# Query halves of an attention kernel kept in the queries' interleaved order and read with a stride, with the order of attention written out anew

## The chip, the cores and the metric

The kernel runs on one core of a Trainium2 chip. The metric is the device time of one execution in microseconds. The core has TensorE (matrix products), VectorE, ScalarE, GpSimd and SyncE (which issues DMAs); in the rows they are PE (PEld for its weight loads), DVE, ACT, POOL and SP. Each engine executes its instructions in the order of the program.

## The reference

Three stages follow one another. The attention is a delta rule with a state S of 48 x 48 for each of 4 x 8 = 32 pairs of batch and head, over 768 steps:

```
k_n = k / (|k| + 1e-6)
for t in range(768):
    y[t] = q[t] @ S
    S = S + beta[t] * outer(k_n[t], v[t] - k_n[t] @ S)
```

Its output, as 3072 tokens of 384 values, goes through a mixture of 8 experts (each token to the best one of them, 384 to 1024 to 384, times its gate), and then through a dense layer 384 to 2048 to 384 with ELU between.

## The kernel before

Attention is cut into 12 chunks of 64 steps. The 32 pairs are taken two at a time: with 64 steps of one pair and 64 of another on the 128 partitions, a pair of pairs u = 0 to 15 is one block-diagonal matrix. Float32 values are split into a float16 high part and a float16 low part (value minus high), and a product is made of three: high x high, high x low, low x high.

For each chunk c the program does this. `lane(c)` scales k, splits it (khi, klo), copies it into the block-diagonal tile bdK, transposes it with TensorE into KTc, copies that into bdKT, makes the masked Gram matrix Lc = KT x KT (`gram`, kind gramL), and copies it into bdL. `invert(g)` inverts the diagonal blocks of two chunks on GpSimd (30 small steps) and puts the result into bdT by DMA. `rest(c)` loads v and q, scales q by 32, splits it into Qc (high and low) and makes the second Gram matrix Ac = KT x Q (`gram`, gramA, plain). `chain(c, hb)` is the recurrence, for each half hb of the pairs: it evicts a residual R into rh (ScalarE or VectorE, kind evac, L1082 or L1083), multiplies by bdT, evicts z, forms the residual with bdL, four times over, and then updates the state. `outputs(c, hb)` copies the state and z into bdS and bdZ, multiplies them with Qc and Ac, and evicts yT; `to_rows` transposes yT into tokens. After every two chunks `route` picks the experts and scatters the tokens with indirect DMAs (GpSimd, L341), 24 in all. After attention the expert stage and the dense layer follow, with a program and an order of their own.

The query tile in SBUF, `raw`, comes with its pairs interleaved: 4 blocks b, 64 steps i, 4 pairs u, u innermost. Qc of before has one contiguous run of 64 steps for each pair, so the split reorders: in `rest` the source is read through `um` with a step of four float32 values. These lines do it (L1320 makes the high half, L1321 the low half on GpSimd, L1323 the scaled low half on VectorE in four instructions):

```
fu = um(q.rearrange("p (b i u) -> p b i u", b=4, u=4))
hi, lo = (Qc[:P112, x].rearrange("p (b u) i -> p b u i", u=4) for x in range(2))
```

TensorE then reads a pair's 64 steps through `un(t, part, u)`, which is contiguous. The other tiles keep an interleave: `at(t, part, u)` reads KTc, Lc, Zc, Sc, bdKT, bdL, bdT with a step of two float16 values, Kc and bdK with a step of four.

The order is written out. Every operation is one of 2,280 entries of a plan. For each there may be several ways (another engine, or a DMA); the string WAYS[kind] has one digit for each operation of the kind, and STARTS has one number for each entry, by which `replay` sorts all entries; each engine then executes its entries in this order, and the four PSUM banks `pw` are handed out in it. So nothing is planned at run time, and the figures of cost beside the operations have no effect on the program while STARTS has as many numbers as there are entries. For the block-diagonal copies (`bd`, two halves each) the digit is 0 for a DMA of SyncE's queue, 1 for VectorE, 2 for ScalarE, 3 for GpSimd. For evac and shi 0 is ScalarE and 1 VectorE. For query the digit picks a triple: who multiplies by 32, who makes the high half, who makes the low half.

Of the kernel before, what the change touches and what calls it, by code (L numbers as in the profile page):

```python
# [199 lines left out]
class Moe(Ops):  # L200
# [92 lines left out]
    def route(self, a, xt, first, step, last):  # L293
# [51 lines left out]
        for b in tiles:  # L345
            x, g = xt[:, b, :DM], self.gs[:, b:b + 1]
            a.op("gate", ("ACT", DM + 155, lambda x=x, g=g: nc.scalar.activation(out=x, in_=x, func=AF.Copy, scale=g)),
                    ("DVE", DM - 130, lambda x=x, g=g: dv.tensor_scalar(out=x, in0=x, scalar1=g, scalar2=None, op0=ALU.mult)), r=["gs"], w=[f"xt{b}"])
            a.pl.add("POOL", 1.04, lambda b=b: scatter(b), r=[f"xt{b}", "di", f"xid{b}", "xz", *xs], move=0.55)
        if not last:  # L350
            xi = xt.bitcast(I32)[:, part, DM]
            a.pl.add("POOL", 0.1, lambda: nc.gpsimd.tensor_scalar(out=xi, in0=xi, scalar1=128, scalar2=None, op0=ALU.add), w=[f"{x}{b}" for b in tiles for x in ("xid", "xt")])
# [600 lines left out]
C = 64  # L953
# [58 lines left out]
class Attn(Ops):  # L1012
# [7 lines left out]
    def __init__(self, ctx, tc, plan, kt, vt, qt, beta, ident, zeros, lend):  # L1020
# [24 lines left out]
        self.Ac, self.Qc = til("Ac", [128, 2, NP, C]), many("Qc", [128, 2, NP, C], NQ)  # L1045
# [46 lines left out]
    def clear(self, names, t, after=(), due=()):  # L1092
# [6 lines left out]
                ("DVE", n, lambda: nc.vector.memset(f, 0.0)),  # L1099
# [66 lines left out]
    def gains(self, c0, c1, keep=False):  # L1166
# [4 lines left out]
        for c in range(c0, c1):  # L1171
            k, kn = self.load_k(c)
            q, qn = k, kn
            if keep:
# [3 lines left out]
                    ("POOL", 874, lambda k=k, q=q: nc.gpsimd.tensor_tensor(out=q, in0=k, in1=k, op=ALU.mult)),  # L1178
# [10 lines left out]
    def bd(self, dst, dn, src, sn, rows, cols=C):  # L1189
# [4 lines left out]
        for h in range(2):  # L1194
# [6 lines left out]
                              ("POOL", 0.185 + m * 0.0012, lambda o=oc, i=ic: nc.gpsimd.tensor_copy(o, i), 0.0)])  # L1201
# [4 lines left out]
    def gram(self, c, dst, dn, mov, mn, kind, plain=False):  # L1206
# [4 lines left out]
        col = un if plain else at  # L1211
        for hb in range(2):
# [24 lines left out]
            buf = self.pe(0.68, prod, r=[*two(f"bdKT{c % NT_}"), *mn], after=[nh, nl], take="pw")  # L1237
# [59 lines left out]
    def rest(self, c):  # L1297
# [14 lines left out]
        fu = um(q.rearrange("p (b i u) -> p b i u", b=4, u=4))  # L1312
        hi, lo = (Qc[:P112, x].rearrange("p (b u) i -> p b u i", u=4) for x in range(2))
        if c == NC_ - 1:
            hi, lo, fu = um(hi), um(lo), um(fu)
# [139 lines left out]
    def outputs(self, c, hb):  # L1455
# [29 lines left out]
        if c:  # L1485
            buf = self.pe(0.68, state, r=["bdSa", "bdSb", *qn, *ar], after=["yT"], take="pw")
# [36 lines left out]
    "bd": "1002000120202202022020110122120110002100001000030000000011022001000201010000000100111000000111000010000002000021100000002303030010000010000130300232030000001011",  # L1523
    "clear": "1012101110132103211200",
    "dg": "000000100110000101100001001000000010000000100000",
    "evac": "000100000100000010000001001000000001010101000110010000001001100000101000000101001001000000100100000011110000000000000010101000000000011101001010110111000010110001011110011110100100000000000001",
    "gate": "000010011010001011111111",
    "gramA": "715064030343250603356405",
    "gramL": "310011071602163015661356",
    "invert": "111111",  # L1530
    "kgain": "000100101110",
    "khi": "000011010010",
    "klo": "010100000001",
    "last": "001000221000220011002100",
    "lput": "111010101001110010111101",
    "norm": "000001100000",
    "query": "212121105515",
    "shi": "1100000000000010011001",
    "square": "002000120011",
    "turn": "101101001000000000101100000000000011000101010010",  # L1540
    "value": "101010121010",
    "whi": "0001011",
    "wlow": "0011000",
    "xput": "100010010100100010001000",
    "xsq": "001000000010100000101000",
# [188 lines left out]
```

## Time and profile before

| | |
|---|---|
| time, median of 3 runs (lowest to highest) | 990.22 us (988.76 to 990.22) |
| the profiled execution: time, span | 988.69 us, 986.9 us |
| TensorE busy | 852.7 us (86% of the span) |
| VectorE busy | 775.1 us (79%) |
| ScalarE busy | 600.0 us (61%) |
| GpSimd busy | 434.8 us (44%) |
| TensorE's granted clock, mean | 0.951 |

The span is the time from the first to the last instruction in the profile; the execution's time lies 1.8 us above it. Busy time is the time in which an engine executes an instruction; waits for semaphores are not in it. The granted clock is a share of TensorE's full speed, 2.4 GHz.

### The profile page before, as it was taken

The numbers are of one execution on the slowest core, as the hardware profiler recorded it, in microseconds if no ns is written. First come the engines' busy times: TensorE is split into PE (matmuls) and PEld (weight loads), VectorE is DVE, ScalarE is ACT, GpSimd is POOL, SyncE is SP. The second block draws the span as 40 slices with busy tenths as digits, with TensorE's granted clock in tenths as the row PEclk, the third lists the DMA queues.
The fourth block names the chain that finished last, engine by engine and source line by source line (L and its number), as shares of the span: only waits on it lengthen the run. The fifth ranks groups of instructions, "written<-read, shape, count | busy, mean of one in ns | idle before, by whom it ended". The sixth has DMA issues, their size and how long they took to land.

```text
span 986.9 us, 28916 instructions
## 1 busy us (share of the span) xinstructions
PE 852.7 (86%) x11783; PEld 711.4 (72%) x11784; DVE 775.1 (79%) x1631; ACT 600.0 (61%) x1077; POOL 434.8 (44%) x635
## 2 busy tenths in 40 slices
PE   0448888788798785699999999989999999999995
PEld 0436786678687674355556566879999999999995
DVE  7887887778687774577899797997778777878874
ACT  9786777767685851465566644765545555555662
POOL 6465464665556322123233421355446362355452
PEclk9957999899899987799999999999999999999998
DMA  6658874747653523967799526401010100100000
GB/s 204 158 117 234 226 154 93 147 110 130 136 112 89 176 65 106 242 141 235 223 222 210 189 80 127 125 18 49 18 49 17 48 19 1 49 17 18 18 17 18
DMA packets 122103, 108.79 MB, mean 110 GB/s; under 512 B 79753, under 2 KB 107181, under 8 KB 121709
## 3 DMA queue, kind: packets, MB, share of 16 engines
q1 hardware_dynamic: 115885, 84.84, 35.5%
q0 software_dynamic: 6080, 22.05, 6.9%
q8 instruction: 94, 1.54, 0.7%
q14 instruction: 44, 0.36, 0.1%
HBM read 74.19 MB, written 19.97 MB: 95 GB/s over the span
## 4 chain that ended last, share of the span: by engine, by line
PE 52%; DVE 4%; issue 2%; DMA 1%; SPq 0%; ACT 0%; POOL 0%; POOLq 0%; ACTq 0%; DVEq 0%
PE pa L648 18%; PE acc L668 15%; PE acc L606 10%; PE pa L587 9%; DMA xr<-xs_scratch 1%; DVE wbl L662 1%; DVE w L512 1%; PE pa L559 0%; PE pa L555 0%; DVE w L511 0%; DVE y L616 0%; DVE wal L654 0%; DVE wbl L466 0%; SPq L542 0%; DVE x L564 0%
## 5 line engine op out<-in xcount | busy, mean ns | idle before, releaser
L668 PE MATMUL acc<-dbh,wbl 128*128 128x192 f16 x672 | 165.3, 246 | 0.0
L668 PE MATMUL acc<-dbh,wbh 128*128 128x192 f16 x672 | 165.3, 246 | 0.0
L668 PE MATMUL acc<-dbl,wbh 128*128 128x192 f16 x672 | 165.3, 246 | 0.0
L648 PE MATMUL pa<-x,dah 128*128 128x256 f16 x1152 | 158.2, 274 | 3.1 <-DVE wal L654 2.5
L648 PEld LDWEIGHTS <-dah 128*128 128x128 f16 x1152 | 112.5, 98 | 16.4 <-issue 3.6
L668 PEld LDWEIGHTS <-wbh 128*128 128x128 f16 x1344 | 122.0, 98 | 1.2
L648 PE MATMUL pa<-x,dal 128*128 128x256 f16 x576 | 95.0, 274 | 0.0
L587 PE MATMUL pa<-x,wah 128*128 128x440 f16 (+6 forms) x384 | 77.5, 338 | 0.6 <-DVE hl L601 0.4
L1204 PEld LDWEIGHTS <-bdKT 112*128 112x128 f16 x1680 | 58.6, 102 | 19.9 <-issue 14.2
L1204 PEld LDWEIGHTS <-bdL 128*128 128x128 f16 x1536 | 55.9, 101 | 21.9 <-issue 15.7
L661 ACT CAST wbh<-wah 128x384 f16<-128x384 f32 (+1 forms) x88 | 49.3, 561 | 34.9 <-PE acc L668 12.0
L600 ACT ACTIVATE hh<-pa 128x440 f16<-128x440 f32 (+6 forms) x64 | 32.1, 505 | 58.3 <-PE acc L606 34.0
L668 PEld LDWEIGHTS <-wbl 128*128 128x128 f16 x672 | 65.7, 98 | 0.1
L1204 PEld LDWEIGHTS <-bdK 128*128 128x128 f16 x960 | 40.9, 119 | 33.6 <-DVE bdK L1200 14.3
L606 PE MATMUL acc<-hh,wbh 128*128 128x440 f16 (+6 forms) x192 | 64.1, 334 | 0.0
L655 POOL TENSOR_TENSOR wal<-wal 128x128 f32<-128x128 f32 (+1 forms) x65 | 43.1, 663 | 47.6 <-DVE wal L655 23.1
L606 PE MATMUL acc<-hl,wbh 128*128 128x440 f16 (+6 forms) x192 | 64.1, 334 | 0.0
L606 PE MATMUL acc<-hh,wbl 128*128 128x440 f16 (+6 forms) x192 | 64.1, 334 | 0.0
L655 POOL TENSOR_TENSOR wah<-wah 128x128 f32<-128x128 f32 (+1 forms) x62 | 37.0, 597 | 58.2 <-DVE wah L655 33.5
L661 ACT CAST wbh<-wal 128x384 f16<-128x384 f32 (+1 forms) x74 | 42.2, 571 | 32.8 <-PE acc L668 16.6
L648 PEld LDWEIGHTS <-dal 128*128 128x128 f16 x576 | 56.7, 98 | 6.9 <-DVE dal L527 0.2
L1204 PE MATMUL R<-z,bdL 128*128 128x48 f16 x1536 | 58.8, 189 | 2.7 <-issue 2.1
(323 smaller groups left out, 2370.3 us busy)
## 6 DMA issues: line engine op xcount, KB each, us to landing
st<-in_w SPq DMA_DIRECT2D x24, 512.0 KB
st<-in_w SPq DMA_DIRECT2D x32, 384.0 KB
kraw<-in_k SPq DMA_DIRECT2D x22, 384.0 KB
w<-in_w_in POOLq DMA_DIRECT2D x12, 512.0 KB, 4.6
w<-in_w_out POOLq DMA_DIRECT2D x16, 384.0 KB, 3.4
xs_scratch<-in_zeros SPq DMA_DIRECT2D x8, 675.5 KB
raw<-in_q SPq DMA_DIRECT2D x12, 448.0 KB
vraw<-in_v SPq DMA_DIRECT2D x12, 384.0 KB
```

Of the source, the lines that this page charges most:

```text
L512: self.dve(n, lambda m=m, lo=lo: v.scalar_tensor_tensor(out=m, in0=lo, scalar=29, in1=m, op0=ALU.logical_shift_right, op1=ALU.bitwise_or), ...
L587: self.nc.tensor.matmul(self.pa[i][:, :n], lhsT=W[w][:, k, c], rhs=x[:, k, y, t0:t0 + n], start=j == 0 and k == 0, stop=j == 2 and k == 2)
L600: self.act(cap, lambda i, hh=hh: nc.scalar.activation(out=hh, in_=self.pa[i][:, :cap], func=AF.Relu), w=[hn], buf=buf)
L606: nc.tensor.matmul(self.acc[d][:, :cap], lhsT=w[:, f, c], rhs=h, start=f == 0 and j == 0, stop=f == 7 and j == 2)
L648: nc.tensor.matmul(o, lhsT=D[w][:, k, c], rhs=x[:, k, y, t0:t0 + 256], start=q + n + k == 0, stop=n + k == 4, skip_group_check=True)
L655: add = lambda o, x, y, op: [(e, n, lambda w=w: w.tensor_tensor(out=o, in0=x, in1=y, op=op)) for e, n, w in (("POOL", o.shape[1] * 128, nc ...
L661: self.op("ghi", ("ACT", n, lambda f=f, fh=fh: nc.scalar.copy(fh, f)), ("DVE", n / 2, lambda f=f, fh=fh: v.tensor_copy(fh, f)), r=[gn + z] ...
L662: self.op("glow", *((e, n * c, lambda f=f, fh=fh, fl=fl, w=w: w.tensor_tensor(out=fl, in0=f, in1=fh, op=ALU.subtract)) for e, c, w in (("D ...
L668: nc.tensor.matmul(self.acc[k][:, o:o + HD], lhsT=h[:, u - 1], rhs=D[d][:, p, w - 1], start=p == 0 and n == 0 and o == FIRST[k], stop=p == ...
L1204: self.nc.tensor.matmul(o, lhsT=l, rhs=r, start=st, stop=True, skip_group_check=True)
```

## The change

Qc keeps the queries' own order, [4 blocks, 64 steps, 4 pairs]. Both halves are then written contiguously, from a contiguous source, and the scaled low half on VectorE is one instruction and not four. TensorE reads a pair's 64 steps at a step of four float16 values, through the new helper `by4`, in gramA (576 products) and in the output products with bdS (528 products). The list of query ways is another: without an own multiplication, with a high half on ScalarE or VectorE; and with one on GpSimd, ScalarE or VectorE, with a low half on GpSimd. The strings WAYS and the numbers STARTS of attention are new throughout; by count the strings say:

| kind | before | after |
|---|---|---|
| bd (160 half copies) | DMA 100, VectorE 31, ScalarE 21, GpSimd 8 | DMA 79, VectorE 32, ScalarE 28, GpSimd 21 |
| query, high half | ScalarE 12 | ScalarE 12 |
| query, low half | GpSimd 9, VectorE 3 (scaled) | GpSimd 8, VectorE 4 (scaled) |
| evac (192) | ScalarE 136, VectorE 56 | ScalarE 143, VectorE 49 |
| shi (22) | ScalarE 16, VectorE 6 | ScalarE 20, VectorE 2 |
| yout (24) | ScalarE 17, VectorE 7 | ScalarE 13, VectorE 11 |
| klo (12) | GpSimd 9, VectorE 3 | GpSimd 7, VectorE 5 |

The first two digits of bd are chunk 0's copies into bdK (before DMA for the second, after ScalarE), the next two those into bdKT. The other edits are figures of cost (such as 1.04 to 1.33 for a scatter). The core of the diff, without the lists of numbers, the strings of the other kinds and most figures of cost:

```diff
@@ -997,6 +997,11 @@
     return t[:, part, u]
 
 
+def by4(t, part, u):
+
+    return t[:, part, u // 4, :, u % 4]
+
+
 def un4(t):
     return t.rearrange("p (b u) i -> p b u i", u=4)
 
...
@@ -1042,7 +1047,7 @@
         self.lent = [f"{n}{x}" for n in ("bdK2", "bdK3", "bdK4", "bdKT0", "bdL0", "bdL1") for x in "ab"]
         self.lent += ["Kch", "Kcl"] + [f"{n}{hb}{x}" for n in ("KTc", "Lc") for hb in range(2) for x in "hl"]
         self.Zc = til("Zc", [128, 8, 2, C, 2])
-        self.Ac, self.Qc = til("Ac", [128, 2, NP, C]), many("Qc", [128, 2, NP, C], NQ)
+        self.Ac, self.Qc = til("Ac", [128, 2, NP, C]), many("Qc", [128, 2, 4, C, 4], NQ)
         self.Sc = many("Sc", [128, 8, 2, C, 2], 2)
         self.vraw = til("vraw", [128, NP, D], F32)
         self.bdS, self.bdZ = (til(n, [128, 4, 2, 128, 2]) for n in ("bdS", "bdZ"))
...
@@ -1208,7 +1213,7 @@
 
         nc, bdKT = self.nc, self.bdKT[c % NT_]
         self.pl.part = (kind, c)
-        col = un if plain else at
+        col = by4 if plain else at
         for hb in range(2):
             hs = slice(4 * hb, 4 * hb + 4)
             us = slice(hb * HB, (hb + 1) * HB)
...
@@ -1234,7 +1239,7 @@
                 mv = um(oh)
                 f = dst[:, hs].rearrange("p b l i u -> p (b l) (i u)")
                 m16 = self.mask.rearrange("p i u -> p (i u)")[:, None, :].to_broadcast([128, 8, 2 * C])
-            buf = self.pe(0.68, prod, r=[*two(f"bdKT{c % NT_}"), *mn], after=[nh, nl], take="pw")
+            buf = self.pe(0.78 if plain else 0.68, prod, r=[*two(f"bdKT{c % NT_}"), *mn], after=[nh, nl], take="pw")
             key = self.pl.number(kind)
             act = lambda o: ("ACT", 512, lambda i: nc.scalar.copy(o, pv(i)))
             dve = lambda o: ("DVE", 512, lambda i: nc.vector.tensor_copy(o, pv(i)))
...
@@ -1309,19 +1314,18 @@
         self.load(lambda: nc.sync.dma_start(out=q, in_=self.qt[c]), 370e3, w=["raw"])
         f = q
 
-        fu = um(q.rearrange("p (b i u) -> p b i u", b=4, u=4))
-        hi, lo = (Qc[:P112, x].rearrange("p (b u) i -> p b u i", u=4) for x in range(2))
-        if c == NC_ - 1:
-            hi, lo, fu = um(hi), um(lo), um(fu)
+        hi, lo = (Qc[:P112, x].rearrange("p b i u -> p (b i u)") for x in range(2))
         by = {"POOL": ("POOL", 1024, lambda: nc.gpsimd.tensor_tensor(out=f, in0=f, in1=self.sx[:P112].to_broadcast([P112, NP * C]), op=ALU.mult)),
               "ACT": ("ACT", 1024, lambda: nc.scalar.activation(out=f, in_=f, func=AF.Copy, scale=SX)),
               "DVE": ("DVE", 512, lambda: nc.vector.tensor_scalar(out=f, in0=f, scalar1=SX, scalar2=None, op0=ALU.mult)),
               "NONE": ("NONE", 0, lambda: None)}
-        high = {"ACT": ("ACT", 2300, lambda: nc.scalar.copy(hi, fu)), "NONE": ("ACT", 2300, lambda: nc.scalar.activation(out=hi, in_=fu, func=AF.Copy, scale=SX))}
-        low = {"POOL": ("POOL", 1310, lambda: nc.gpsimd.tensor_tensor(out=lo, in0=fu, in1=hi, op=ALU.subtract)),
-               "DVE": ("DVE", 1930, lambda: nc.vector.tensor_tensor(out=lo, in0=fu, in1=hi, op=ALU.subtract)),
-               "NONE": ("DVE", 1930, lambda: [nc.vector.scalar_tensor_tensor(out=lo[:, b], in0=fu[:, b], scalar=SX, in1=hi[:, b], op0=ALU.mult, op1=ALU.subtract) for b in range(4)])}
-        ways = [(by[a], high["NONE" if a == "NONE" else "ACT"], low[b]) for a, b in (("POOL", "POOL"), ("ACT", "POOL"), ("NONE", "NONE"), ("POOL", "DVE"), ("ACT", "DVE"), ("DVE", "POOL"), ("DVE", "DVE"))]
+        high = {"ACT": ("ACT", 1024, lambda: nc.scalar.copy(hi, f)), "DVE": ("DVE", 512, lambda: nc.vector.tensor_copy(hi, f)),
+                "NACT": ("ACT", 1024, lambda: nc.scalar.activation(out=hi, in_=f, func=AF.Copy, scale=SX)),
+                "NDVE": ("DVE", 512, lambda: nc.vector.tensor_scalar(out=hi, in0=f, scalar1=SX, scalar2=None, op0=ALU.mult))}
+        low = {"POOL": ("POOL", 1024, lambda: nc.gpsimd.tensor_tensor(out=lo, in0=f, in1=hi, op=ALU.subtract)),
+               "DVE": ("DVE", 1024, lambda: nc.vector.tensor_tensor(out=lo, in0=f, in1=hi, op=ALU.subtract)),
+               "N": ("DVE", 1024, lambda: nc.vector.scalar_tensor_tensor(out=lo, in0=f, scalar=SX, in1=hi, op0=ALU.mult, op1=ALU.subtract))}
+        ways = [(by[a], high[b], low[d]) for a, b, d in (("NONE", "NACT", "N"), ("NONE", "NDVE", "N"), ("POOL", "ACT", "POOL"), ("ACT", "ACT", "POOL"), ("DVE", "ACT", "POOL"), ("POOL", "DVE", "POOL"), ("ACT", "DVE", "POOL"), ("DVE", "DVE", "POOL"))]
         key = self.pl.number("query")
         for k, kw in enumerate((dict(r=["sx"], w=["raw"]), dict(r=["raw"], w=[qn + "h"]), dict(r=["raw", qn + "h"], w=[qn + "l"]))):
             self.op(None, *(w[k] for w in ways), key=key, **kw)
...
@@ -1474,7 +1478,7 @@
         def state(i):
             for n in range(HB):
                 for k, (a, b) in enumerate(parts):
-                    mm(col(i, n), at(bdS, a, n)[:P112], un(Qc, b, hb * HB + n)[:P112], n == 0 and k == 0)
+                    mm(col(i, n), at(bdS, a, n)[:P112], by4(Qc, b, hb * HB + n)[:P112], n == 0 and k == 0)
 
         def inner(i):
             for n in range(HB):
...
@@ -1483,7 +1487,7 @@
 
         ar = [*zn, f"Ac{hb}h", f"Ac{hb}l"]
         if c:
-            buf = self.pe(0.68, state, r=["bdSa", "bdSb", *qn, *ar], after=["yT"], take="pw")
+            buf = self.pe(0.78, state, r=["bdSa", "bdSb", *qn, *ar], after=["yT"], take="pw")
             self.pe(0.68, inner, r=ar, buf=buf)
         else:
             buf = self.pe(0.68, inner, r=ar, after=["yT"], take="pw")
...
@@ -1520,112 +1524,112 @@
 PP = 9
 
 WAYS = {
...
-    "bd": "1002000120202202022020110122120110002100001000030000000011022001000201010000000100111000000111000010000002000021100000002303030010000010000130300232030000001011",
-    "evac": "000100000100000010000001001000000001010101000110010000001001100000101000000101001001000000100100000011110000000000000010101000000000011101001010110111000010110001011110011110100100000000000001",
+    "bd": "1222000220202202222220112122120130002110321001033000000010020001230201010000000100111000001231010010000020000003300010111333300030000010001323012133210030031033",
+    "evac": "000000000000000010000001000000001000110111000100010000001001100010101000000101101011000000010010000011000000100000000101100000001000001101001011010000000000000010001110011110100100000000000100",
-    "klo": "010100000001",
-    "query": "212121105515",
-    "shi": "1100000000000010011001",
-    "yout": "000110000001100010110000",
+    "klo": "110100000011",
+    "query": "030303320434",
+    "shi": "0100000000000000000001",
+    "yout": "011110000111100010011000",
 }
 STARTS = (
...
 )
```

## Rows read from the trace of the kernel before

**Rows 1.** Stretches: us, busy time and count of each engine, granted clock, DMA share, GB/s.

```profile
78.00:378.00 300.00, 247.82 (x6205) 221.84 (x6204) 231.37 (x547) 208.84 (x430) 152.38 (x249) 0.93 0.57 134
393.00:987.00 594.00, 567.84 (x5076) 459.59 (x5076) 475.95 (x932) 327.40 (x577) 233.38 (x292) 0.98 0.33 90
```

**Rows 2.** The query: groups by line, instructions of tile Qc, one burst in the timeline.

```profile
L1321 POOL TENSOR_TENSOR Qc<-raw,Qc 112x1024 f16<-112x1024 f32 x9 | 26.2, 2909 | 16.7 <-ACT Qc L1320 16.7
L1320 ACT CAST Qc<-raw 112x1024 f16<-112x1024 f32 x9 | 21.9, 2429 | 3.7 <-PE pw L1204 3.6
L1323 DVE SCALAR_TENSOR_TENSOR Qc<-raw,Qc 112x256 f16<-112x256 f32 x12 | 6.7, 623 | 0.4 <-ACT Qc L1320 0.4
L1320 ACT ACTIVATE Qc<-raw 112x1024 f16<-112x1024 f32 x3 | 6.3, 2092 | 0.3 <-DMA raw<-in_q 0.2
...
L1204 PE MATMUL pw<-Qc,bdKT x576: 189/193/242, 43.0 to 366.2; 112*128 112x64 f16 x192
L1204 PE MATMUL pw<-Qc,bdS x528: 189/193/204, 117.1 to 372.5; 112*128 112x64 f16 x176
...
239.54 0.86 PE L1204 MATMUL pw<-Qc,bdKT 112*128 112x64 f16 x24
```

**Rows 3.** Groups by line: the expert stage's split of contiguous weights.

```profile
L477 POOL TENSOR_TENSOR wal<-st,wah 128x1024 f16<-128x1024 f32 x9 | 20.5, 2275 | 29.0 <-ACT wah L476 26.7 <-DVE wbl L466 2.2
L466 DVE SCALAR_TENSOR_TENSOR wal<-st,wah 128x1024 f16<-128x1024 f32 x15 | 19.2, 1294 | 0.1
L465 ACT ACTIVATE wah<-st 128x1024 f16<-128x1024 f32 x10 | 10.8, 1085 | 0.0
```

**Rows 4.** Timeline at 248 us: start, duration, engine, line, what, count.

```profile
247.65 0.61 PEld L1204 LDWEIGHTS <-bdK 128*128 128x128 f16 x16
...
249.87 0.47 PEld L1204 LDWEIGHTS <-bdKT 112*128 112x128 f16 x16
```

**Rows 5.** Timeline around a query high half on ScalarE.

```profile
240.25 2.12 ACT L1320 CAST Qc<-raw 112x1024 f16<-112x1024 f32 x1
...
240.97 0.56 PE L1204 MATMUL R<-z,bdL 128*128 128x48 f16 x16
...
242.28 0.48 ACT L1082 ACTIVATE rh<-R 128x384 f16<-128x384 f32 x1
...
242.81 0.56 DVE L1083 TENSOR_SCALAR z<-pw 128x384 f16<-128x384 f32 x1 [1.16 <-ACT rh L1082]
```

**Rows 6.** Timeline: VectorE's dg scalings beside GpSimd.

```profile
138.04 2.48 DVE L1083 TENSOR_SCALAR dg<-Lc 32x512 f16<-32x512 f16 x3
138.06 2.01 POOL L1201 COPY bdL<-Lc 64x2048 f16<-64x2048 f16 x1
...
220.12 2.66 POOL L1321 TENSOR_TENSOR Qc<-raw,Qc 112x1024 f16<-112x1024 f32 x1 [0.29 <-ACT Qc L1320]
220.65 2.46 DVE L1083 TENSOR_SCALAR dg<-Lc 32x512 f16<-32x512 f16 x1
...
254.90 0.29 DVE L1083 TENSOR_SCALAR dg<-Lc 32x512 f16<-32x512 f16 x1
```

**Rows 7.** Timeline of the start.

```profile
14.40 2.04 ACT L1320 ACTIVATE Qc<-raw 112x1024 f16<-112x1024 f32 x1 [0.21 <-DMA raw<-in_q]
...
18.14 0.82 ACT L1270 CAST Kc<-kraw 128x768 f16<-128x768 f32 x1
...
19.04 1.65 POOL L1089 TENSOR_TENSOR Kc<-kraw,Kc 128x768 f16<-128x768 f32 x1
...
27.36 1.87 PE L1204 MATMUL pw<-i,bdK 128*128 128x64 f16 x32 [13.29 <-DMA bdK<-Kc]
```

**Rows 8.** Groups by line: block-diagonal copies.

```profile
L1200 ACT COPY bdK<-Kc 64x1536 f16<-64x1536 f16 x4 | 5.9, 1466 | 0.3 <-POOL Kc L1089 0.3
L1201 POOL COPY bdZ<-Zc 64x768 f16<-64x768 f16 x4 | 3.3, 823 | 4.1 <-DVE lgp L1514 4.1
```

**Rows 9.** Waits from 78 to 378 us: us in total, times, longest.

```profile
PEld L1204 <- DMA bdS<-Sc: 4.5, 2, 3.0
```

More of the change, by code (lines that the diff above doesn't have):

```diff
@@ L348, in route @@
                     ("DVE", DM - 130, lambda x=x, g=g: dv.tensor_scalar(out=x, in0=x, scalar1=g, scalar2=None, op0=ALU.mult)), r=["gs"], w=[f"xt{b}"])
-            a.pl.add("POOL", 1.04, lambda b=b: scatter(b), r=[f"xt{b}", "di", f"xid{b}", "xz", *xs], move=0.55)
+            a.pl.add("POOL", 1.33, lambda b=b: scatter(b), r=[f"xt{b}", "di", f"xid{b}", "xz", *xs], move=0.55)
         if not last:
             xi = xt.bitcast(I32)[:, part, DM]
-            a.pl.add("POOL", 0.1, lambda: nc.gpsimd.tensor_scalar(out=xi, in0=xi, scalar1=128, scalar2=None, op0=ALU.add), w=[f"{x}{b}" for b in tiles for x in ("xid", "xt")])
+            a.pl.add("POOL", 0.25, lambda: nc.gpsimd.tensor_scalar(out=xi, in0=xi, scalar1=128, scalar2=None, op0=ALU.add), w=[f"{x}{b}" for b in tiles for x in ("xid", "xt")])
     def finish_routing(self, a):
@@ L1098, in clear @@
                 ("ACT", n, lambda: nc.scalar.activation(out=f.rearrange("p (a b) -> p a b", b=128), in_=z, func=AF.Copy, scale=0.0)),
-                ("DVE", n, lambda: nc.vector.memset(f, 0.0)),
+                ("DVE", n * 0.755, lambda: nc.vector.memset(f, 0.0)),
                 ("LD", n * 260, lambda: nc.sync.dma_start(out=f, in_=self.zeros[:, :n].to_broadcast([128, n]))), w=names, after=after, r=due)
@@ L1177, in gains @@
             self.op("square", ("ACT", 768, lambda k=k, q=q: nc.scalar.activation(out=q, in_=k, func=AF.Square)),
-                    ("POOL", 874, lambda k=k, q=q: nc.gpsimd.tensor_tensor(out=q, in0=k, in1=k, op=ALU.mult)),
+                    ("POOL", 680, lambda k=k, q=q: nc.gpsimd.tensor_tensor(out=q, in0=k, in1=k, op=ALU.mult)),
                     ("DVE", 768, lambda k=k, q=q: dv.tensor_tensor(out=q, in0=k, in1=k, op=ALU.mult)), r=[kn], w=[qn])
@@ L1200, in bd @@
                         ways=[("DVE", d0 + m / 4 * d1, lambda o=oc, i=ic: nc.vector.tensor_copy(o, i), 0.0), ("ACT", a0 + 0.025 + m * a1, lambda o=oc, i=ic: nc.scalar.copy(o, i), 0.0),
-                              ("POOL", 0.185 + m * 0.0012, lambda o=oc, i=ic: nc.gpsimd.tensor_copy(o, i), 0.0)])
+                              ("POOL", 0.185 + m * 0.00089, lambda o=oc, i=ic: nc.gpsimd.tensor_copy(o, i), 0.0)])
     def mm(self, o, l, r, st):
@@ L1542 @@
[L1542 to L1545, printed above, removed]
-    "yout": "000110000001100010110000",
-    "zhi": "10101000100000000001100000",
+    "bd": "1222000220202202222220112122120130002110321001033000000010020001230201010000000100111000001231010010000020000003300010111333300030000010001323012133210030031033",
+    "clear": "1011131213212201000330",
+    "dg": "100100000100000111110001010000000010000010000000",
+    "evac": "000000000000000010000001000000001000110111000100010000001001100010101000000101101011000000010010000011000000100000000101100000001000001101001011010000000000000010001110011110100100000000000100",
@@ new lines @@
+    "gate": "000100010111110110111101",
+    "gramA": "105754011335267665044455",
+    "gramL": "310001051002116615661360",
+    "invert": "111111",
+    "kgain": "001100001110",
+    "khi": "000011100010",
+    "klo": "110100000011",
+    "last": "001000201010000011000100",
+    "lput": "000110000100100100010100",
+    "norm": "000020100001",
+    "query": "030303320434",
+    "shi": "0100000000000000000001",
+    "square": "002000120012",
+    "turn": "010101000011000001100010000001000011101001000100",
@@ L1548 @@
+    "value": "101010122010",
+    "whi": "0010011",
+    "wlow": "0000101",
+    "xput": "101100010000000000001000",
+    "xsq": "000000001010100000101000",
+    "yout": "011110000111100010011000",
+    "zhi": "10101000100000000000100000",
 }
 STARTS = (
[79 rows of a table removed]
[79 rows of a table added]
 )
```

13 lines of the change are left out of this document (removed), and 158 rows, old and new, of the table STARTS.

## The prediction, made blind

> **What bounds the kernel now.** I first cut the span at 78 and 378 us with the table of stretches [rows 1]. The change touches only what lies before about 385 us (attention and routing); the 594 us from 393 on are 60% of the span, have TensorE busy 568 us, and their code is unedited. I leave them as they are. So the question is by how much attention ends earlier or later; a microsecond there is a microsecond of the whole.
>
> Between 78 and 378 us, in 300 us, TensorE is busy 248 (83%), VectorE 231 (77%), ScalarE 209 (70%), GpSimd 152 (51%) [rows 1]. No engine is full. Every one follows a fixed order and the recurrence runs through three of them, so TensorE is the nearest to a bound and the rest of its time goes in waits. Next I read the groups by line for the query's instructions [rows 2], then rows elsewhere in the trace that already do what the new form does [rows 3], then the timeline around one query high half [rows 5], one GpSimd copy [rows 6] and the start [rows 7], and last the list of waits for the block-diagonal DMAs [rows 9].
>
> **The high halves.** Today ScalarE takes 21.9 us for nine and 6.3 for three, 28.2 in all [rows 2]. The new form is a plain copy of 1024 contiguous values to half precision. The MoE weights have exactly that, one float32 tile in, one float16 tile out, at 1.085 us [rows 3]. 12 x 1.085 = 13.0, so ScalarE is given back 15.2 us.
>
> **The low halves.** GpSimd now does nine in 26.2 us; VectorE does three, as 12 quarter instructions of 0.623, 7.5 us [rows 2]. The new strings give GpSimd eight and VectorE four. The same subtraction on a contiguous weight tile takes 2.275 on GpSimd and the scaled one 1.294 on VectorE [rows 3]: 18.2 and 5.2. So GpSimd -8.0, VectorE -2.3.
>
> **The strided reads.** 576 and 528 products read a query half [rows 2], 1104 in all, and each now takes its 64 columns at a step of four float16 values, 8 bytes. No product of before moves data at that step; the nearest row is a weight load. bdK is laid out with the same step: 16 loads of it take 0.61 us, 16 of bdKT, whose step is two values, 0.47 [rows 4]. That is 8.8 ns more for 128 columns, 4.4 for 64: 1104 x 4.4 = +4.8 us on TensorE. Lower bound 0 (a strided read has no way to beat a contiguous one). Upper bound: each column costs two, which would double a product; 24 of them take 0.86 us, 36 ns each [rows 2], so at most +40 us. I take 4.8, as the bdK row is the same step on the same engine. TensorE is busy 83% here and part of its work fills gaps, so the end gets 0.83 x 4.8 = +4.0 us. Three whole-bank subtracting products fewer in the new strings give perhaps a microsecond back; I take +3.
>
> The rule that bears on this is in the Trainium skill, SBUF — State Buffer (section Door 1, the note on cachelines): two hits within a 16-byte line keep full bandwidth, so 8 half-precision values can be spanned freely. By it the 8-byte step costs nothing and this term is -1 in place of +3. The bdK row speaks against it, on the weights' side; no row shows the moving side, so it stays as a rival below.
>
> **Where ScalarE's 15 us go.** Not to the end directly: the new strings fill them. Seven block-diagonal copies move to it (a copy into bdK takes 1.47 us [rows 8], and three small, three like it and one larger come: some 9 us), seven evictions of the recurrence come from VectorE (7 x 0.48 = 3.4 [rows 5]), the rest is small change both ways. ScalarE ends about 3 us lighter or even. VectorE loses seven evictions, 7 x 0.56 = 3.9, and the 2.3 above; the other moves (outputs, row and logit copies, state halves, low parts of k) go both ways and I count them as cancelling: -6. For an engine at 77% with short queues I give the end a sixth of that: -1.
>
> **The shorter block in ScalarE's order.** ScalarE works in order, so a recurrence eviction behind a high half waits for all of it. At 240.25 us a high half occupies it for 2.12. TensorE's residual for the other half-chain ended at 241.53, the eviction rh starts only at 242.28, VectorE's z then waits 1.16 us for it [rows 5]. With 1.085 ScalarE would be free at 241.3, before the residual ends: 0.75 us off that half-chain. TensorE had other work and lost only a part of this. I take 0.3 us of the end for each of the ten or so high halves that lie in the steady stage: -3. Bounds: 0 (another order may put it where nothing is behind it) and 10 x 1.0 = -10.
>
> **The start.** Before the first eviction chain can run, chunk 0 has to pass k's high part, low part, copy into bdK, transposes. The first query high half (14.40, 2.04 us) stands ahead of k's high part (18.14) on ScalarE, and the low part follows on GpSimd (19.04, 1.65) [rows 7]. The change takes 0.96 off the first. TensorE's first transposes start at 27.36 us after 13.29 us idle, ended by the DMA of a half of bdK [rows 7]; the new string gives that half to ScalarE, after the low part (over at 20.7), at 1.47 us [rows 8]. So the transposes could start about 4.5 us earlier. But chunk 1 keeps such a DMA and the first inverse needs both chunks, so I take a third: -1.5 (bounds 0 and -4.5).
>
> **Fewer DMAs.** 21 of 100 block-diagonal DMAs go. In the steady stage TensorE's weight loads waited 4.5 us for bdS by DMA [rows 9]; a fifth of it is -1 (bounds 0 and -4.5). The DMA's own traffic is not a limit here, at 57% [rows 1].
>
> **GpSimd against VectorE.** 13 copies go to GpSimd (0.82 us for the smallest [rows 8], 2.01 for the largest [rows 6]). Here the trace shows a price: while GpSimd copied bdL at 138.06 (2.01 us), three dg scalings that take 0.29 each [rows 6] took 2.48 together, so one was held 1.6 us [rows 6]. Behind a query low half at 220.12 another was held to 2.46 us [rows 6]. Eight copies cost VectorE at least that 1.6 us, 0.2 each: 13 more cost +2.6. Low halves shorter by a fifth return about 1.4. Half of the net reaches the end: +0.6. Upper bound: each new copy holds VectorE for 80% of its mean length of 1.05 us, as the one at 138 did, 13 x 0.84 = 10.9.
>
> This agrees with the Trainium skill, SBUF — State Buffer (section A bandwidth-pool intuition that's wrong): GpSimd and a VectorE operation that uses both of its ports block each other fully, rather than share. By the rule, every copy may hold one such operation to its end, which is the upper bound just given; the rule makes this a rival.
>
> **Sum.** +3 - 1 - 3 - 1.5 - 1 + 0.6 = -2.9 us. The profiled execution took 988.69 (span 986.9), so it would be 985.8. The median of the runs is 990.22, 1.5 above the profiled one; the forecast for the median is 990.22 - 2.9 = **987.3 us**.
>
> **What the sum leaves out.** The order is written out anew over all 2,280 entries, so each engine's neighbours change. Where TensorE pauses, how long its clock then stays at the lower of its levels, 1.2 in place of 2.4 GHz (granted 0.93 of full speed on average here [rows 1]), and which VectorE instruction meets which GpSimd instruction is settled by it. Two identical sums with other orders could differ by several us. This, more than any term, sets the width.
>
> **Rivals.**
> *A: no change* (0.24). The recurrence and TensorE at 83% set the pace, the high halves had cover (TensorE lost little at 240 us), the start's gain is eaten by chunk 1's DMA and by the routing's scatters, which stay 24. For it: ScalarE's freed time is filled again. Time: +3 - 1 - 1 - 1 = 0, so 990.
> *B: GpSimd's copies hold VectorE* (0.17), the one on the other side. Place: dg scalings and VectorE's own copies, in the chunks where the string has a 3. With 10.9 - 1.4 = 9.5 us on VectorE, of which now 80% reach the end because VectorE becomes the late one: 7.6 in place of 0.6, sum +4.1, 994.3. It decides once a copy holds VectorE by about 0.5 us on average (13 x 0.5 x 0.8 = 5.2, less 1.4, against the -3.5 of the others). Against it: of eight copies I found one long hold.
> *C: the strided read costs double* (0.05): 0.83 x 40 - 1 = +32 in place of +3, sum +26, 1016. It beats the gains from about 8 ns a product (0.83 x 1104 x 8 ns = 7.3 us, against -5.9 for the rest).
> *D: the 8-byte step is free* (0.08): term -1 in place of +3, sum -6.9, 983.3. It is what the page's note on cachelines would give.
> *E: the new order makes longer TensorE pauses, so more time at the lower clock* (0.06): each 0.01 of granted clock over 300 us is 3 us: 0.02 lower gives +3, 993.
> *Forecast* (0.40): 987.3, between 984 and 988.2.
>
> Faster by over 0.2% (2 us; about what a measurement of this kernel tells from none) holds the forecast and D: 0.48. Same is A: 0.24. Slower is B, C and E: 0.28. The range goes from 981 (D with the start's full gain) to 994.5 (B); C, part of B and E, and an order that happens to be better than any sum, 0.2 together, lie beyond. The forecast's own range is 984 to 990.
>
> **What would show it.** High halves near 1.09 us and low halves near 2.3 and 1.3. 24 query products in 0.96 us or so, not 0.86 (D) or 1.7 (C). The first transposes near 23 to 25 us. Attention's last products about 3 us earlier. Held dg scalings: few, or many (B). Granted clock between 78 and 375 at 0.93 or under (E). The prediction is wrong if the MoE part changes length, or if attention's end moves by more than the terms while each of them is as forecast: then the order did it.

## The result, and the profile after

| | before | after |
|---|---|---|
| time, median (lowest to highest) | 990.22 us (988.76 to 991.57, 4 runs) | 999.26 us (998.15 to 999.93, 3 runs) |
| ratio, 95% interval | | 1.0101 [1.0063, 1.0138] |
| profiled execution, span | 986.9 us | 996.1 us |

The changed kernel is about 10 us slower; 987.3 was forecast, and the range ended at 994.5. One further execution of it took 2951.93 us and is left out here and in the ratio; with it the median is 999.6 us.

The first view to read is again the table of stretches, of the kernel after (columns as in [rows 1]): the same 300 us of attention, the expert and dense stages, and then the same program cut at the end of the last product of Qc with bdS, at 384.7 us.

```profile
78.00:378.00 300.00, 269.01 (x6039) 244.96 (x6036) 213.24 (x479) 196.79 (x432) 157.46 (x256) 0.92 0.53 126
400.00:996.00 596.00, 568.62 (x5120) 461.74 (x5117) 475.88 (x932) 327.50 (x577) 233.67 (x293) 0.98 0.34 92
24.00:384.70 360.70, 303.11 (x6589) 274.65 (x6588) 264.56 (x596) 245.33 (x492) 186.67 (x301) 0.89 0.54 126
384.70:996.10 611.40, 577.16 (x5192) 468.28 (x5189) 483.28 (x979) 331.23 (x591) 238.70 (x301) 0.98 0.34 91
```

The kernel before, cut at its own last such product:

```profile
24.00:372.70 348.70, 271.85 (x6596) 241.87 (x6597) 271.56 (x612) 247.43 (x469) 179.30 (x289) 0.91 0.59 138
372.70:986.90 614.20, 580.05 (x5191) 469.36 (x5188) 484.18 (x986) 330.86 (x592) 238.76 (x301) 0.97 0.34 91
```

All of the loss lies in attention: +12.0 us up to that product, -2.8 after it. TensorE executes almost the same number of products (6589 for 6596) but is busy 31.3 us longer. VectorE became 7.0 us and ScalarE 2.1 us lighter. TensorE's time without work fell from 76.9 (348.7 - 271.85) to 57.6 us, so 19.3 us of the extra work are made up for by shorter pauses and 12.0 us made attention longer. The two kernels also differ in their order, so this doesn't yet say what the strided reads alone cost; the second group of experiments does.

The groups by line name the products. In the kernel before (the query's other groups are in [rows 2]):

```profile
L1204 PE MATMUL pw<-Qc,bdKT 112*128 112x64 f16 x576 | 21.9, 197 | 0.0
L1204 PE MATMUL pw<-Qc,bdS 112*128 112x64 f16 x528 | 19.0, 193 | 2.3 <-DMA bdS<-Sc 1.4 <-DVE Lc L1246 0.9
```

and in the kernel after:

```profile
L1209 PE MATMUL pw<-Qc,bdKT 112*128 112x64 f16 x576 | 39.6, 240 | 2.8 <-issue 2.1 <-ACT KTc L1288 0.8
L1209 PE MATMUL pw<-Qc,bdS 112*128 112x64 f16 x528 | 35.7, 241 | 0.4 <-ACT lgp L1518 0.4
L1325 POOL TENSOR_TENSOR Qc<-raw,Qc 112x1024 f16<-112x1024 f32 x8 | 17.1, 2143 | 11.9 <-ACT Qc L1322 11.9
L1322 ACT CAST Qc<-raw 112x1024 f16<-112x1024 f32 x8 | 8.4, 1049 | 2.9 <-PE pw L1209 2.8
L1327 DVE SCALAR_TENSOR_TENSOR Qc<-raw,Qc 112x1024 f16<-112x1024 f32 x4 | 4.8, 1203 | 0.0
L1323 ACT ACTIVATE Qc<-raw 112x1024 f16<-112x1024 f32 x4 | 4.2, 1058 | 2.1 <-PE pw L1209 2.0
```

Its timeline: the first transposes, and the last output products.

```profile
23.84 1.87 PE L1209 MATMUL pw<-i,bdK 128*128 128x64 f16 x32 [12.81 <-DVE bdK L1205]
...
379.02 1.60 PE L1209 MATMUL pw<-Qc,bdS 112*128 112x64 f16 x24
383.10 1.64 PE L1209 MATMUL pw<-Qc,bdS 112*128 112x64 f16 x24
```

The query's own instructions did what was forecast: a high half (the plain copy) takes 1.05 us in the mean and no longer 2.43 (one of those nine took 4.90), a low half 2.14 on GpSimd and 1.20 on VectorE. But 24 products with a query half take 1.60 to 1.64 us where they took 0.86. The two groups of products sum to 75.3 us against 21.9 + 19.0 = 40.9 in the kernel before for the same stretch: the 31 us of TensorE, and a little more.

### The profile page after: what moved, and what is told of

The parts are those of the page before. It is cut to its first block, busy times and chain, and to the rows that moved or that the text cites. A ratio compares the mean times of both kernels' runs of the same rounds, so it can differ in the third digit from the quotient of the medians.

```text
span 996.1 us, 28882 instructions
## 1 busy us (share of the span) xinstructions
PE 881.2 (88%) x11777; PEld 743.3 (75%) x11778; DVE 766.4 (77%) x1607; ACT 597.9 (60%) x1102; POOL 439.6 (44%) x647
## 4 chain that ended last, share of the span: by engine, by line
PE 51%; DVE 5%; issue 2%; DMA 1%; SPq 0%; ACT 0%; POOL 0%; POOLq 0%; ACTq 0%
PE pa L648 17%; PE acc L668 15%; PE acc L606 10%; PE pa L587 9%; DMA xr<-xs_scratch 1%; DVE wbl L662 1%; DVE w L512 1%; PE pa L559 0%; DVE wal L654 0%; PE pa L555 0%; DVE w L511 0%; DVE wah L655 0%; DVE wal L655 0%; DVE dbl L527 0%; DVE y L616 0%
## 5 line engine op out<-in xcount | busy, mean ns | idle before, releaser
L648 PEld LDWEIGHTS <-dah 128*128 128x128 f16 x1152 | 111.9, 98 | 16.7 <-issue 4.3
L1209 PEld LDWEIGHTS <-bdKT 112*128 112x128 f16 x1680 | 74.6, 107 | 26.3 <-issue 21.9
L587 PE MATMUL pa<-x,wah 128*128 128x440 f16 (+6 forms) x384 | 76.9, 337 | 0.6 <-DVE hl L601 0.4
L661 ACT CAST wbh<-wah 128x384 f16<-128x384 f32 (+1 forms) x88 | 49.3, 561 | 34.6 <-PE acc L668 11.9
L655 POOL TENSOR_TENSOR wal<-wal 128x128 f32<-128x128 f32 (+1 forms) x65 | 43.0, 662 | 47.7 <-DVE wal L655 23.2
L661 ACT CAST wbh<-wal 128x384 f16<-128x384 f32 (+1 forms) x74 | 42.2, 571 | 32.0 <-PE acc L668 16.7
```

The lines of the kernel that those rows point to most:

```text
L587: self.nc.tensor.matmul(self.pa[i][:, :n], lhsT=W[w][:, k, c], rhs=x[:, k, y, t0:t0 + n], start=j == 0 and k == 0, stop=j == 2 and k == 2)
L648: nc.tensor.matmul(o, lhsT=D[w][:, k, c], rhs=x[:, k, y, t0:t0 + 256], start=q + n + k == 0, stop=n + k == 4, skip_group_check=True)
L655: add = lambda o, x, y, op: [(e, n, lambda w=w: w.tensor_tensor(out=o, in0=x, in1=y, op=op)) for e, n, w in (("POOL", o.shape[1] * 128, nc ...
L661: self.op("ghi", ("ACT", n, lambda f=f, fh=fh: nc.scalar.copy(fh, f)), ("DVE", n / 2, lambda f=f, fh=fh: v.tensor_copy(fh, f)), r=[gn + z] ...
L1209: self.nc.tensor.matmul(o, lhsT=l, rhs=r, start=st, stop=True, skip_group_check=True)
```

## The experiments

They form four groups, each on a chip of its own. The kernel before took 961 to 1000 us in them, so ratios to the runs of the kernel before on the same chip are compared, and profiles only within one group. The quoted texts are the expectations, written before the runs; their absolute times belong to the 990.22 us of the first chip.

**First group: forms and order apart.** The change has three parts: contiguous writes of the query halves, strided reads by TensorE, and a new order with new engine choices. "Contiguous" below means that the queries lie pair by pair in DRAM already, so that writes and reads are both contiguous; against the changed kernel that is

```diff
-    return t[:, part, u // 4, :, u % 4]
+    return t[:, part, u]
...
-        self.Ac, self.Qc = til("Ac", [128, 2, NP, C]), many("Qc", [128, 2, 4, C, 4], NQ)
+        self.Ac, self.Qc = til("Ac", [128, 2, NP, C]), many("Qc", [128, 2, NP, C], NQ)
...
-        hi, lo = (Qc[:P112, x].rearrange("p b i u -> p (b i u)") for x in range(2))
+        hi, lo = (Qc[:P112, x].rearrange("p u i -> p (u i)") for x in range(2))
...
-    qp = np.zeros((NC_, 2, C, 4, C, 4), np.float32)
+    qp = np.zeros((NC_, 2, C, 4, 4, C), np.float32)
-    qp[:, :, :D] = cut(q).transpose(3, 2, 5, 0, 4, 1)
+    qp[:, :, :D] = cut(q).transpose(3, 2, 5, 0, 1, 4)
```

*Strided, old order* (the changed kernel, with the strings and numbers of the kernel before; each query triple replaced by the one with the same engines):

```diff
-    "query": "030303320434",
+    "query": "030303324434",
-    "bd": "1222000220202202...",
+    "bd": "1002000120202202...",
```

> The changed kernel's query halves (contiguous writes, reads at a step of four values) in the order and with the engine choices of the kernel before. Theory 1 (the strided read doubles TensorE's 1104 query products, +36 us of TensorE work, less than half of which reaches the end): slower than before by 8 to 16 us, 998 to 1006. Theory 2 (the new order is what costs: other pauses, other collisions, lower clock): within 3 us of before, 987 to 993.

*Contiguous, new order* (the diff above, alone):

> The changed kernel with its new order, but the queries laid out pair by pair in DRAM, so that both the writes of the halves and TensorE's reads are contiguous; every instruction and its place stay. Theory 1: 24 query products back at 0.86 us, the time falls by 12 to 18 us to 982 to 988. Theory 2: it stays at 996 to 1000.

*Contiguous, old order* (both of these diffs):

> The same contiguous queries in the order and with the engine choices of the kernel before: what the shorter high and low halves alone are worth. Both theories: 984 to 990 (my terms for the shorter ScalarE block and the start say 3 to 4 us faster than before).

*Old forms, new order* (the kernel before with the new strings and numbers, the same engines for each query):

```diff
-    "query": "212121105515",
+    "query": "212121102515",
-    "bd": "1002000120202202...",
+    "bd": "1222000220202202...",
```

> The new order with the split as it was before (strided source, pair by pair in SBUF, contiguous reads by TensorE): the order alone. Theory 1: 985 to 992, no worse than before. Theory 2: 997 or more.

| | ratio, 95% interval | median, us |
|---|---|---|
| kernel before | 1 | 968.36 |
| strided, old order | 1.019 [1.0144, 1.0235] | 986.82 |
| contiguous, old order | 0.9999 [0.9967, 1.003] | 968.43 |
| contiguous, new order | 0.9941 [0.9914, 0.9968] | 962.48 |
| old forms, new order | 1.0058 [1.0027, 1.0088] | 975.03 |

With the order of before held, the step alone costs 986.82 - 968.43 = 18.4 us. Groups by line, the strided one in the old order first and the contiguous one in the old order below it:

```profile
L1209 PE MATMUL pw<-Qc,bdKT 112*128 112x64 f16 x576 | 38.8, 240 | 0.2 <-DVE Lc L1248 0.2
L1209 PE MATMUL pw<-Qc,bdS 112*128 112x64 f16 x528 | 35.7, 240 | 0.0
```

```profile
L1209 PE MATMUL pw<-Qc,bdKT 112*128 112x64 f16 x576 | 20.9, 193 | 1.3 <-issue 0.8 <-DVE lgp L1518 0.4
L1209 PE MATMUL pw<-Qc,bdS 112*128 112x64 f16 x528 | 19.0, 193 | 1.2 <-DMA bdS<-Sc 1.0 <-ACT rh L1087 0.2
```

That is 74.5 against 39.9: 34.6 us more on TensorE, of which 18.4 (53%) reach the end. Without the step the change as a whole is a gain. One part of it without the other is none: short query halves in the old order show no gain (0.9999, with an interval of 3 us to either side), and the new order with the long halves costs 0.6%.

Measured from the kernel before on each chip, two expectations of the first theory were missed. The strided reads in the old order lost 18.5 us, where 8 to 16 were expected, and more than half of TensorE's extra work reached the end. The old forms in the new order lost 6.7 us, where a gain of 5 to a loss of 2 was expected; that is nearly the 7 us which the second theory asked for there, so the new order is not free when it stands alone.

**Second group: the changed kernel beside its contiguous twin, a smaller step, and GpSimd's copies.**

*The changed kernel again:*

> The changed kernel itself, on one chip with the three that follow. If the strided reads alone make the changed kernel slow, it stands about 1.6% above the same kernel with contiguous reads, so a ratio of 1.010 to kernel before. If the gap between the two seen so far came from the two chips they ran on, both have ratios within 0.4% of each other.

*Contiguous, new order, again:*

> The changed kernel's order with queries that lie pair by pair (contiguous writes, contiguous TensorE reads). Strided reads as the cause: ratio 0.994 to kernel before, as seen, and 24 products of Qc with bdS in 0.86 us. Chips as the cause: the same ratio as the changed kernel.

*A step of two* (queries interleaved by two pairs, everything else as in the changed kernel):

```diff
-    return t[:, part, u // 4, :, u % 4]
+    return t[:, part, u // 2, :, u % 2]
...
-        self.Ac, self.Qc = til("Ac", [128, 2, NP, C]), many("Qc", [128, 2, 4, C, 4], NQ)
+        self.Ac, self.Qc = til("Ac", [128, 2, NP, C]), many("Qc", [128, 2, 8, C, 2], NQ)
...
```

> The changed kernel with queries interleaved by two pairs in place of four: the writes stay contiguous, TensorE reads every second float16 value (4 bytes). If only a step of 8 bytes costs (the products of KTc, which have the step of two, take 0.88 us for 24), then 24 query products take 0.86 to 0.89 us, TensorE is 30 us less busy before the experts than with the step of four, and the ratio is 0.994 to 0.997. If the price grows in proportion to the step, 24 products take about 1.1 us, and the ratio lies near 1.000.

*Fewer GpSimd copies* (contiguous, new order; 17 digits of bd that the change made a 3 are those of before again):

```diff
-    "bd": "...2122120130002110321001033000..."
+    "bd": "...2122120110002110021001030000..."
```

> Contiguous queries and the new order, but the 17 block-diagonal copies that the change moved to GpSimd go back to where they were (8 to VectorE, 8 to DMAs, 1 to ScalarE). If GpSimd's copies hold VectorE (rival B: 0.84 us each and 80% of it to the end, 17 x 0.84 x 0.8 = 11 us, less about 5 us for the 8 that VectorE now makes itself), it gets faster: ratio about 0.988 to kernel before. If they hide behind other work, it does not gain: 0.994 or a little more, up to 1.000 where a DMA that lands later is waited for.

| | ratio, 95% interval | median, us |
|---|---|---|
| kernel before | 1 | 992.08 |
| changed kernel | 1.0124 [1.0084, 1.0163] | 1004.19 |
| contiguous, new order | 0.9889 [0.9853, 0.9925] | 981.03 |
| step of two | 0.9867 [0.9824, 0.9909] | 980.86 |
| fewer GpSimd copies | 0.9901 [0.9863, 0.9939] | 984.08 |

The changed kernel and the contiguous one differ in nothing but the step at which TensorE reads and the layout that goes with it, and lie 23.2 us apart, so the step costs more than the whole loss. Stretches up to the end of the last product of Qc with bdS, then the groups, in the changed kernel:

```profile
24.00:385.50 361.50, 298.96 (x6589) 270.71 (x6590) 266.38 (x597) 245.35 (x493) 188.14 (x301) 0.92 0.53 126
```

```profile
L1209 PE MATMUL pw<-Qc,bdKT 112*128 112x64 f16 x576 | 39.6, 240 | 1.8 <-issue 1.8
L1209 PE MATMUL pw<-Qc,bdS 112*128 112x64 f16 x528 | 35.7, 241 | 1.1 <-ACT lgp L1518 1.1
```

and in the contiguous one:

```profile
24.00:363.00 339.00, 268.54 (x6591) 239.41 (x6589) 264.08 (x596) 243.21 (x490) 190.70 (x301) 0.91 0.57 135
...
78.00:378.00 300.00, 251.32 (x6230) 223.88 (x6227) 226.49 (x551) 204.25 (x459) 168.63 (x268) 0.93 0.56 132
```

```profile
L1209 PE MATMUL pw<-Qc,bdKT 112*128 112x64 f16 x576 | 23.8, 196 | 6.6 <-issue 5.9 <-ACT KTc L1288 0.7
L1209 PE MATMUL pw<-Qc,bdS 112*128 112x64 f16 x528 | 18.9, 193 | 1.4 <-ACT lgp L1518 1.4
```

This closes the account. The strided groups cost 75.3 - 42.7 = 32.6 us more; TensorE as a whole is busy 30.4 us longer; its time without work shrinks from 70.5 to 62.5 us, so 8 us of the extra work lie in former pauses; 22.5 us remain, and attention ends 22.5 us later. (Of the 19.3 us of pauses that vanished between the first two profiles, the larger part therefore isn't the step's doing.) Why more of the step reaches the end in this order (22.5 of 30.4) than in the old one (18.4 of 34.6) stays open. At a step of two a burst is back to

```profile
363.61 0.89 PE L1209 MATMUL pw<-Qc,bdS 112*128 112x64 f16 x24
```

and the time is that of the contiguous kernel. The writes are contiguous there too and their source is interleaved, so neither the writes nor the interleave as such cost anything that shows: only the distance of 8 bytes between the values that TensorE reads does. Both of these versions beat both kernels.

GpSimd's copies: with 17 fewer, GpSimd is busy 21 us less and VectorE 2.2 us more in the same 300 us,

```profile
78.00:378.00 300.00, 251.62 (x6224) 224.64 (x6223) 228.71 (x555) 205.63 (x461) 147.68 (x248) 0.93 0.56 133
```

and the time is the same within the intervals. They hide behind other work; rival B is out as a cause of 10 us. The swap also gave VectorE eight copies and SyncE eight DMAs, so a hold of a microsecond or two in sum could still be masked.

**Third group: the price by step** (one run, with a step for each chunk):

```diff
+STEP = (4, 1, 2, 4, 8, 16, 1, 2, 4, 8, 16, 1)
+def by(t, part, u, n):
+    return t[:, part].rearrange("p (b i u) -> p b i u", u=n, i=C)[:, u // n, :, u % n]
...
-        col = by4 if plain else at
+        col = (lambda t, p, u: by(t, p, u, STEP[c])) if plain else at
...
```

> A look at TensorE alone: each chunk's queries have a step of their own, for the chunks 0 to 11 steps of 4, 1, 2, 4, 8, 16, 1, 2, 4, 8, 16, 1 float16 values (2 to 32 bytes); writes stay contiguous. If a column costs double as soon as the step exceeds 4 bytes and no more after that, 24 query products take 0.86 us at 1, 0.88 at 2, and 1.6 to 1.7 at 4, 8 and 16. If the price goes with the distance, they take about 3.2 us at 8 and 6 at 16. If it goes with the share of a 16-byte piece that is used, 8 and 16 are alike and well above 4.

From its timeline, one burst of 24 products each for the chunks 0 to 5 (steps of 4, 1, 2, 4, 8, 16 values):

```profile
40.01 1.60 PE L1211 MATMUL pw<-Qc,bdKT 112*128 112x64 f16 x24
...
91.81 0.86 PE L1211 MATMUL pw<-Qc,bdKT 112*128 112x64 f16 x24
...
116.97 0.88 PE L1211 MATMUL pw<-Qc,bdKT 112*128 112x64 f16 x24
...
159.00 1.61 PE L1211 MATMUL pw<-Qc,bdKT 112*128 112x64 f16 x24
...
165.17 2.96 PE L1211 MATMUL pw<-Qc,bdKT 112*128 112x64 f16 x24
...
203.47 3.00 PE L1211 MATMUL pw<-Qc,bdKT 112*128 112x64 f16 x24
...
226.48 3.01 PE L1211 MATMUL pw<-Qc,bdS 112*128 112x64 f16 x24
```

36, 37, 67, 123 and 125 ns a product for 1, 2, 4, 8 and 16 values. The first expectation (double and no more) and the second (with the distance, without end) both miss; the third fits: the price goes up 1.8 times from 4 to 8 bytes and again from 8 to 16, and 32 bytes cost about what 16 do. A reading that fits all five steps is that the number of wanted values among the eight of a 16-byte piece counts: with four or eight there is hardly a price, with two a product takes nearly twice, with one over three times as long. Steps between these five were not run, so it is a reading and not the only one.

The granted clock matters here. The first five bursts ran at 1.00 (2.4 GHz), the sixth at 0.50 (1.2 GHz). The last line is an output burst of chunk 5, at the same step of 16 values and at a clock of 1.00, and takes as long as the sixth, so the halved clock did not make that one slower. The 8-byte step behaves alike: in the changed kernel bursts at 0.50 (at 139.97, 179.04 and 210.42 us) took 1.61 to 1.63 us, those at 1.00 1.60 to 1.64. Contiguous bursts took 1.45 to 1.47 us at 0.50 (kernel before at 94.22 and 180.22 us, contiguous kernel of the second group at 204.69 us) and 0.86 at 1.00. So the step costs about 0.75 us a burst at the full clock and about 0.15 at the lower one.

The run as a whole took 996.2 us against 965.39 for the kernel before beside it, one run each.

**Fourth group: where the gain of the rest comes from.** All three are contiguous, in the new order.

*The base:*

> The contiguous queries in the new order once more, as the base for the two beside it: ratio 0.989 to 0.994 to kernel before, as seen on two chips.

*The start by DMA* (the second half of chunk 0's bdK):

```diff
-    "bd": "1222000220202202...",
+    "bd": "1022000220202202...",
```

> Contiguous queries in the new order, with one copy undone: the second half of chunk 0's bdK goes by DMA again and not by ScalarE. If the start reaches the end as forecast (a third of 4.5 us), the first transposes begin at about 27 us, 3.5 us later than without it, and the time is 1.5 us longer (ratio +0.0015); if all of it reaches the end, 3.5 to 4.5 us longer (+0.004); if later waits swallow it, no difference.

*Block-diagonal copies as before* (all of bd; 48 of 160 digits differ):

```diff
-    "bd": "1222000220202202...",
+    "bd": "1002000120202202...",
```

> Contiguous queries in the new order, with all 160 block-diagonal half copies on the engines and DMAs of kernel before (48 digits differ). The prediction gives them 1.5 (start) + 1 (fewer DMAs) - 0.6 = about 2 us of the gain: ratio +0.002 over the base. If the new order was laid out around them and they are the larger part of the gain, the gain goes wholly: ratio 1.000 or above. If the gain lies in the shorter query halves and the other choices, no difference from the base.

| | ratio, 95% interval | median, us |
|---|---|---|
| kernel before | 1 | 967.58 |
| base | 0.9919 [0.9887, 0.9951] | 960.79 |
| start by DMA | 0.989 [0.9842, 0.9938] | 959.1 |
| copies as before | 1.006 [1.0027, 1.0094] | 975.84 |

The start copy makes no difference that can be measured; with intervals of 3 to 5 us, the 1.5 us of the forecast could not have been seen. It was also a weak test: TensorE's first transposes moved by 0.9 us only, not by 3.5, from

```profile
24.53 1.87 PE L1209 MATMUL pw<-i,bdK 128*128 128x64 f16 x32 [12.79 <-DVE bdK L1205]
```

in the base to

```profile
25.42 1.87 PE L1209 MATMUL pw<-i,bdK 128*128 128x64 f16 x32 [14.01 <-DMA bdK<-Kc]
```

The copies as a whole are worth 15 us in this order. Stretches of the base, cut at its last product with bdS, and three of its waits (us in total, times, longest; from 24 to 361 us in both kernels):

```profile
24.00:342.60 318.60, 259.56 (x6591) 233.73 (x6592) 265.80 (x597) 243.21 (x491) 192.74 (x301) 0.93 0.61 143
```

```profile
POOL raw L1318 <- DMA raw<-in_q: 5.2, 1, 5.2
POOL vraw L1312 <- DMA vraw<-in_v: 4.8, 2, 3.0
...
POOL kraw L1094 <- DMA kraw<-in_k: 3.6, 2, 2.0
```

and with the copies as before:

```profile
24.00:361.20 337.20, 265.47 (x6589) 238.40 (x6590) 265.47 (x595) 236.44 (x484) 174.81 (x288) 0.92 0.62 143
```

```profile
POOL vraw L1312 <- DMA vraw<-in_v: 10.2, 4, 5.0
...
POOL kraw L1094 <- DMA kraw<-in_k: 9.3, 3, 4.6
POOL raw L1318 <- DMA raw<-in_q: 8.4, 1, 8.4
...
PE pw L1209 <- DMA bdS<-Sc: 4.9, 2, 3.9
...
PEld L1209 <- DMA bdS<-Sc: 4.0, 1, 4.0
PE pw L1209 <- DMA bdZ<-Zc: 3.6, 2, 2.1
```

Attention ends 18.6 us later; TensorE's time without work grows from 59.0 to 71.7 us, and its own work takes 5.9 us longer. The loads of k, q and v go through the same SyncE queue as the block-diagonal DMAs; GpSimd waits 27.9 us for them in these rows and not 13.6. TensorE itself waits for bdS and bdZ by DMA, 4.9 and 3.6 us for products and 4.0 for weights; the base has no such row. How much of the 18.6 us goes through which of these waits was not separated. Nor is it shown that the number of DMAs counts: the 48 digits also move copies between the engines, in an order that was laid out around the other choices. That 17 of the 48 could go back without a measurable loss (second group) shows only that those alone are not the costly ones.

## Why the prediction was wrong

**The step that failed is the size of one term, "The strided reads".** It took the extra 4.4 ns of a weight load whose step is the same 8 bytes [rows 4] for the price of 64 moving columns read at that step. The measured price is (75.3 - 40.9) / 1104 = 31 ns a product between the two first profiles, seven times as much. The upper bound named there, a doubling (+40 us), was near: 34.4 us. The bdK row was the same engine and step, but not the same operand, and did not carry over.

The row was also misread. In the kernel before, between the two lines of [rows 4], stands this one:

```profile
248.21 0.61 PEld L1204 LDWEIGHTS <-bdL 128*128 128x128 f16 x16
```

bdL is read at a step of two values, like bdKT, and 16 of its loads take the 0.61 us of bdK. So the difference of 0.14 us between bdK and bdKT can't be put down to the step, and no run here gives the step's price for weights.

Of the 30 us or so on TensorE, 74% (22.5 of 30.4) reach the end in the new order, where 83% was assumed. TensorE's busy share was no ground for that factor, as the 53% of the old order show, but it was not the mistake that decided.

**Rival C was the right mechanism**, at a chance of 0.05. Its point of decision, 8 ns a product, was passed by far. Its 1016 us were too many: its +32 measured 23, and the other terms gave -11 on the chip with both kernels, where it had -5.9.

**The rest of the sum has the right sign and about the right size, but not for the reasons given.** Without the step the change was forecast at -5.9 us. The contiguous kernel in the new order stands at 0.9941, 0.9889 and 0.9919, so -6 to -11 us. On the one chip that ran both, -11.1 and the 23.2 us of the step make the +12.1 us of the changed kernel. That the other terms came near is luck, as the list shows. (The forecast's own range is written once as 984 to 988.2 and once as 984 to 990; the measured time lies outside both.)

- High and low halves: right, 1.05 for 1.085, 2.14 and 1.20 for 2.275 and 1.294. VectorE -7.0 for -6, ScalarE -2.1 for "3 lighter or even".
- The shorter block on ScalarE, -3: by itself it shows no gain, since the old order with short halves is at 0.9999; the interval [0.9967, 1.003] just reaches -3 us. In the new order the short halves are worth 975.03 - 962.48 = 12.5 us. The trace of before showed the eviction behind the long half [rows 5], but not that an order could make so much more, or nothing, of it.
- Fewer DMAs, -1: not separated. All copy choices together, engines and DMAs, are worth 15 us in this order. The one wait that was priced [rows 9] is only a part of what grew when the copies went back: the loads that share the queue grew too.
- The start, -1.5: the first transposes began at 23.84, inside the 23 to 25 us forecast and 3.5 us earlier than [rows 7]. One copy alone moves them by 0.9 us on one chip and nothing at the end, so the term is not supported.
- GpSimd against VectorE, +0.6: no cost found; B is refuted as the decisive mechanism. The dg scalings, which were to show it, are held about as before: 32 of Lc take 16.7 us on VectorE in the changed kernel, 35 took 16.2. The 1.4 us given back and the mean copy of 1.05 us in that term have no row. The Trainium skill, SBUF — State Buffer (section A bandwidth-pool intuition that's wrong) has GpSimd and a VectorE operation that uses both ports block each other fully. The run with 17 fewer copies shows no gain (0.9901 against 0.9889), so such holds, where they occur, cost the end nothing that could be measured.
- D, a free step: refuted, 1.60 us against 0.86. The Trainium skill, SBUF — State Buffer (section Door 1, the note on cachelines) gives a 16-byte line and asks for two hits in it. The 16-byte piece agrees with the runs; the two hits do not, for TensorE's moving operand: with two of eight values a product takes 67 ns against 36 at the full clock, and 37 with four.
- E, the clock: the first two profiles have 0.91 before and 0.89 after over attention, but on one chip the changed kernel was granted 0.92 and the faster contiguous one 0.91. So it does not explain the 23.2 us.
- The expert stage did not change (568.62 us of TensorE in 596, as in [rows 1]), as assumed.

## What to carry to other kernels

Moving a stride from a few wide element-wise copies to TensorE's reads multiplies it by every product that reads the data: here 15 us of ScalarE were bought with 33 us of TensorE. If an interleave must be read by TensorE, keep it at 4 bytes in float16; that was as fast here as a layout in DRAM in which neither side strides (0.9867 against 0.9889). When a price isn't in the trace, a row of a similar but other operand isn't evidence enough to stay near it, and a difference between two rows is only the price of the step if nothing else differs: where the bound decides the sign, give the bound its chance, and measure that one operation first.

## What the runs showed of the hardware

- TensorE's moving operand in float16, 64 columns, at a granted clock of 1.00: 36 ns a product at a step of 2 bytes, 37 at 4, 67 at 8, 123 at 16, 125 to 127 at 32.
- At a granted clock of 0.50 the contiguous product takes 60 to 61 ns, but the one at 8 bytes 67 to 68 and the one at 32 bytes 125, as at 1.00: the lower clock hides most of the price of the 8-byte step.
- The same kernel differs between chips by more than the change: the contiguous one took 981.03 us on one and 960.79 on another, and its last product with bdS ended at 363.0 and at 342.6 us.
